# Full 128x128 weight blocks for every matmul of the routing in an mLSTM, expert and GLU kernel

## The chip, the cores and the metric

One NeuronCore of one Trainium2 chip runs the whole program. The metric is the device time in microseconds (us). Engines are named as the profile names them: PE is TensorE's matmuls, PEld its weight loads, DVE VectorE, ACT ScalarE, POOL GpSimd, SP SyncE, which issues most DMAs.

## The reference

Three steps follow one another. A gated recurrence (4 batches, 8 heads, 768 steps, head size 40) gives 3072 tokens of 320 values. Each token is then given to one of 8 experts by a greedy rule over all 3072 x 8 gate values, at most 384 tokens to an expert, and goes through that expert's two layers. A gated block follows (320 to 1536 and back).

```python
# recurrence, per head: C = f*C + i*v k^T;  n = f*n + i*k;  y = sigmoid(o) * (C q) / max(|n.q|, 1)
logits = x @ w_gate                      # 3072 x 8
for idx in np.argsort(-logits.flatten()):
    tok, e = idx // 8, idx % 8
    if assigned[tok] >= 0 or counts[e] >= 384:
        continue
    assigned[tok] = e; counts[e] += 1
for e in range(8):
    out[mask_e] = np.maximum(x[mask_e] @ w1[e], 0) @ w2[e]
return ((1 / (1 + np.exp(-(out @ w_gate2)))) * (out @ w_val)) @ w_out
```

## The kernel before, in words

The recurrence runs first, in chunks of 128 steps, in an order that a list scheduler settles. From the line `ctx.enter_context(tc.manual_schedule())` on, each engine's instructions stand in the order in which the code issues them.

**The experts** follow in the order in which they fill up (`Ffn.run(i)`, i = 0 to 7). Each works on the 384 tokens of one expert: first layer, ReLU, second layer, then twelve blocks of the gated part. Nearly all of it is fp32r matmuls with 128x128 weight blocks and 384 or 320 moving columns (lines 966 to 1084), which the rows show as f32.

**The routing** of expert i+1 (`Routing.phase`) is a generator that `drive` advances by one step at each `yield` of `Ffn.run(i)`. Its matmuls so stand between the fp32r matmuls of the expert before it. Phase 0, which has no expert to stand in, runs by itself between the recurrence and the first expert.

A phase looks for a threshold digit by digit, 6, 6, 5, 5, 5 and 5 bits (`BITS`). For each digit, DVE compares all 3072 best gate values (`v`, 128 partitions x 24) with n thresholds, n = 63 or 31 (`compare`, L547), into `cmp`, bf16. PE counts by 24 accumulating matmuls, one for each of the 24 token columns: weights `cmp[:, jj, :n]`, 128 rows and n columns, moving operand `A[:, jj, :]`, 8 columns (L602). DVE turns the counts into a 0/1 column `sat` of n rows, and one matmul with weights `ones[:n, :]` sums it for all partitions (L611). When the threshold is found, one matmul with `ones` counts (L639), five turn the tokens of the expert into a list (L669 to L674: weights `zx`, `md`, `prev` of 48 columns, then `tris` and `ones` of 128), and three gather it by a one-hot matrix `oh` of 48 rows (L694). L716 updates the counts, with `ones`.

So a phase has two blocks of 24 matmuls with 63 weight columns, four with 31, six single ones with 63 or 31 weight rows, a group of five (three in phase 7), a group of three, and L639 and L716, whose weights are 128x128.

Of the kernel before, what the change touches and what calls it, by code (L numbers as in the profile page):

```python
# [7 lines left out]
FT = mybir.dt.float32  # L8
FR = mybir.dt.float32r
BF = mybir.dt.bfloat16  # L10
F16 = mybir.dt.float16
I32 = mybir.dt.int32
# [3 lines left out]
OP = mybir.AluOpType  # L16
# [7 lines left out]
NJ = NC * B  # L24
NT = B * S
E = 8
CAP = NT // E
# [13 lines left out]
class Attention:  # L41
# [325 lines left out]
    def run(self, rt, fn):  # L367
        rt.consts()
        with self.tc.tile_pool(name="a_gate", bufs=1) as self.gp:
            self.setup()  # L370
            self.setup2()
            g1 = self.gates(1, NC)
            self.step(-1, lambda n: None)
            self.step(0, lambda n: [next(g1, 0) for _ in range(2 * n)])
            for _ in g1:
                pass
            self.step(1, lambda n: None)
            self.lambdas()
        with self.tc.tile_pool(name="a_conv", bufs=1) as cv:
            side = fn.prep_moe2(cv)  # L380
            for j in range(2, NC * NS + 1):
                self.step(j, lambda n: [next(side, 0) for _ in range(n)])
            for _ in side:
                pass
# [59 lines left out]
class Routing:  # L444
# [7 lines left out]
    def alloc(self, ctx):  # L452
        self.wk = ctx.enter_context(self.tc.tile_pool(name="r_work", bufs=1))
        self.idx = ctx.enter_context(self.tc.tile_pool(name="r_idx", bufs=2))

    def consts(self):
        nc, one = self.nc, self.one
        jp = self.g["jp"]
# [5 lines left out]
        nc.vector.memset(self.ones, 1.0)  # L464
        it = one.tile([128, 64], I32, name="it64")
        nc.gpsimd.iota(it, pattern=[[1, 64]], base=0, channel_multiplier=0)
        nb, s, self.tab = 0, 32, []
        for r, nb in enumerate(self.BITS):
            s -= nb
            n = 2 ** nb - 1  # L470
            t = one.tile([128, n], I32, name=f"tab{r}")
            nc.vector.tensor_scalar(t, it[:, 1:1 + n], s, None, op0=OP.logical_shift_left)
            self.tab.append((n, s, t))
        n, s, t = self.tab[0]
        k = one.tile([128, 2, n], I32, name="k0")
        self.sign(k[:, 0], t)
# [3 lines left out]
                       allow_small_or_imprecise_dtypes=True)  # L480
        nc.gpsimd.iota(self.we[:, 1], pattern=[[1, E]], base=0, channel_multiplier=0,
                       allow_small_or_imprecise_dtypes=True)
        self.srow = one.tile([48, CAP], F16, name="srow")
        nc.gpsimd.iota(self.srow, pattern=[[1, CAP]], base=0, channel_multiplier=0,
                       allow_small_or_imprecise_dtypes=True)
        self.scol = one.tile([128, 3], FT, name="scol")
        nc.gpsimd.iota(self.scol, pattern=[[128, 3]], base=0, channel_multiplier=1,
                       allow_small_or_imprecise_dtypes=True)
        self.GI = one.tile([48, 129], F16, name="GI")
        jc = one.tile([48, 2], FT, name="jc")  # L490
        nc.gpsimd.iota(jc[:, 0:1], pattern=[[0, 1]], base=0, channel_multiplier=1,
                       allow_small_or_imprecise_dtypes=True)
        nc.vector.tensor_scalar(jc[:, 1:2], jc[:, 0:1], float(NJ), -float(NJ), op0=OP.is_equal, op1=OP.mult)
        nc.vector.tensor_scalar(jc[:, 0:1], jc[:, 0:1], 0.0, None, op0=OP.is_gt)
        nc.vector.tensor_add(self.GI[:, 128:129], jc[:, 0:1], jc[:, 1:2])
        self.mmp = one.tile([128, 2 * NJ + 1], BF, name="mmp")
        nc.vector.memset(self.mmp[:, 0:1], 0.0)
        self.lm = one.tile([128, NJ, E], FT, name="lm")
        self.v = one.tile([128, NJ], FT, name="v")
        self.t8 = one.tile([128, NJ], FT, name="t8")  # L500
        self.A = one.tile([128, NJ, E], BF, name="A")
        self.cmp = one.tile([128, NJ, 63], BF, name="cmp")
        self.pen = one.tile([128, E], FT, name="pen")
# [40 lines left out]
    def compare(self, sl, th, n):  # L544
        v = self.v[:, sl]
        k = v.shape[1]
        self.nc.vector.tensor_tensor(self.cmp[:, sl, :n], v[:, :, None].to_broadcast([128, k, n]),  # L547
                                     th.bitcast(FT)[:, None, :].to_broadcast([128, k, n]), op=OP.is_ge)
# [8 lines left out]
    def phase(self, i, on_e, on_x):  # L557
# [13 lines left out]
        ge = wk.tile([63, E], BF, name="ge")  # L571
        sat = wk.tile([63, 1], BF, name="sat")
        tx = wk.tile([128, 1], I32, name="tx")
        h = 16
        for r, (n, s, tab) in enumerate(self.tab):
# [25 lines left out]
            for jj in range(NJ):  # L601
                nc.tensor.matmul(p[:n, :E], cmp[:, jj, :n], A[:, jj, :], start=(jj == 0), stop=(jj == NJ - 1))  # L602
            if i:
# [6 lines left out]
            p2 = self.ps(i)  # L610
            nc.tensor.matmul(p2[:, :1], self.ones[:n, :], sat[:n], start=True, stop=True)  # L611
            dig = wk.tile([128, 1], U32, name="dig", bufs=2)
# [37 lines left out]
        nc.vector.tensor_reduce(mx, es, axis=AX.X, op=OP.max)  # L650
        mm = self.mmp[:, 1:]
        zx = wk.tile([128, 2 * NJ], BF, name="zx")
        md = wk.tile([128, 2 * NJ], BF, name="md")
        nc.vector.tensor_scalar(mm[:, :NJ], self.asg, mx, None, op0=OP.is_equal)
# [13 lines left out]
        po, pk = p[:48, 128:129], p[:, 132:132 + NJ]  # L668
        nc.tensor.matmul(po, zx, self.ones[:, :1], start=True, stop=True)  # L669
        nc.tensor.matmul(p[:48, :128], md, self.tri, start=True, stop=False)  # L670
        nc.tensor.matmul(p[:48, :128], prev, self.ones, start=False, stop=True)
        if not last:
# [3 lines left out]
        gi = self.GI  # L676
        oh = wk.tile([48, CAP], F16, name="oh")
        nc.vector.tensor_copy(off, po)
        nc.vector.tensor_scalar(oh, self.srow, off, None, op0=OP.is_ge)
        nc.vector.tensor_copy(gi[:, :128], p[:48, :128])  # L680
        if not last:
# [39 lines left out]
class Ffn:  # L721
# [208 lines left out]
    def trans(self, i):  # L930
        nc, xg = self.nc, self.XG.pop(i)

        def tr(p, tb, d):
            r0, n = ROWS[d]
            nc.tensor.transpose(p[:n, tb * 128:(tb + 1) * 128], xg[:, tb, r0:r0 + n], self.g["ident"])

        if i:
            def src(d):
                p = self.mmt()[:, :CAP]
                for tb in range(3):  # L940
                    tr(p, tb, d)
                return p
        else:
            R = self.g["R"]
            ps = [self.ps.tile([128, CAP], FT, name=f"ac{d}", bufs=1) for d in range(3)]
            for tb in range(3):
                pw = self.g["rps"](1)[:, :504]
                for _ in range(WARM[tb]):
                    nc.tensor.matmul(pw, R.ones, R.cmp[:, :8, :], start=True, stop=True)
                for d in range(3):  # L950
                    tr(ps[d], tb, d)

            def src(d):
                return ps[d]
        self.XH[i] = []
        yield from self.split("x", src, self.XH[i])
        if self.padfree:
            self.widen(self.XH[i])
        else:
            self.owed = self.XH[i]  # L960
# [151 lines left out]
def tile_kernel(ctx, tc, a, out):  # L1112
    nc = tc.nc
# [3 lines left out]
    g = {}  # L1117
    g["jp"] = con.tile([128, 128], FT, name="jp")
    nc.gpsimd.iota(g["jp"], pattern=[[1, 128]], base=0, channel_multiplier=-1, allow_small_or_imprecise_dtypes=True)
    g["ident"] = con.tile([128, 128], FT, name="ident")  # L1120
    nc.vector.tensor_scalar(g["ident"], g["jp"], 0.0, None, op0=OP.is_equal)
    g["lg"] = con.tile([128, NJ, E], FT, name="lg")
# [3 lines left out]
    with ExitStack() as c2:  # L1126
        at = Attention(c2, tc, g, a, xd)
        at.run(r, fn)
    fn.alloc(ctx)
# [53 lines left out]
```

## Time and profile before

| | |
|---|---|
| median of three runs (lowest, highest) | 911.55 us (905.52, 912.48) |
| the profiled execution: time, span | 911.91 us, 910.2 us |
| granted TensorE clock, mean of the span | 0.947 of full speed |
| busy: PE, PEld, DVE, ACT, POOL | 94%, 89%, 62%, 39%, 31% |
| recurrence | 0 to 223 us of the span |
| routing phase 0, alone, clock 0.5 | 223 to 251 us |
| experts 0 to 7, clock 1.0 | 251 to 906 us |

The busy shares are means over stages of different kinds. The time itself lies about 1.7 us over the span. A clock of 1.0 is 2.4 GHz, 0.5 is 1.2 GHz.

### The profile page before, as it was taken

The numbers are of one execution on the slowest core, as the hardware profiler recorded it, in microseconds if no ns is written. First come the engines' busy times: TensorE is split into PE (matmuls) and PEld (weight loads), VectorE is DVE, ScalarE is ACT, GpSimd is POOL, SyncE is SP. The second block draws the span as 40 slices with busy tenths as digits, with TensorE's granted clock in tenths as the row PEclk, the third lists the DMA queues.
The fourth block names the chain that finished last, engine by engine and source line by source line (L and its number), as shares of the span: only waits on it lengthen the run. The fifth ranks groups of instructions, "written<-read, shape, count | busy, mean of one in ns | idle before, by whom it ended". The sixth has DMA issues, their size and how long they took to land.

```text
span 910.2 us, 16439 instructions
## 1 busy us (share of the span) xinstructions
PE 854.9 (94%) x6284; PEld 808.6 (89%) x6284; DVE 562.9 (62%) x1492; ACT 356.7 (39%) x753; POOL 281.0 (31%) x295
## 2 busy tenths in 40 slices
PE   6899798988499999999999999999999999999996
PEld 5898787988289999999999999999998999999996
DVE  7869999796765656655555565556555555542321
ACT  6498756551043251243215224422522341243321
POOL 3356676552120071044007103500720170053001
PEclk9698789797599999999999999999999999999999
DMA  6987878550130130040031005001300400060000
GB/s 123 188 191 153 194 169 178 124 142 30 38 113 1 39 111 23 1 149 23 2 112 38 23 1 150 22 2 56 94 23 1 136 30 8 1 149 23 1 1 22
DMA packets 125215, 65.64 MB, mean 72 GB/s; under 512 B 103888, under 2 KB 115344, under 8 KB 125136
## 3 DMA queue, kind: packets, MB, share of 16 engines
q1 hardware_dynamic: 122688, 56.68, 26.4%
q0 software_dynamic: 2304, 7.87, 2.7%
q8 instruction: 49, 0.80, 0.4%
q14 instruction: 30, 0.25, 0.1%
q10 hardware_dynamic: 144, 0.05, 0.0%
HBM read 56.71 MB, written 7.86 MB: 71 GB/s over the span
## 4 chain that ended last, share of the span: by engine, by line
PE 73%; DVE 6%; DMA 1%; issue 1%; POOL 1%; ACT 1%; SPq 0%; POOLq 0%; DVEq 0%; ACTq 0%
PE mm L966 8%; PE mm L968 7%; PE mm L967 7%; PE mm L988 7%; PE ac L1082 5%; PE mm L973 5%; PE mm L972 5%; PE ac L1084 5%; PE ac L1083 4%; PE rp L602 3%; PE ac L1005 3%; PE ac L1006 2%; PE ac L1007 2%; PE po L296 1%; PE ac L1011 1%
## 5 line engine op out<-in xcount | busy, mean ns | idle before, releaser
L926 POOL DMA_INDIRECT xg<-xd,ix x24 | 23.8, 993 | 399.4 <-DVE scr L697 394.6
L966 PE MATMUL mm<-yh,mh 128*128 128x384 f32 x384 | 135.1, 352 | 0.0
L967 PE MATMUL mm<-yh,ml 128*128 128x384 f32 x384 | 130.1, 339 | 0.0
L968 PE MATMUL mm<-yl,mh 128*128 128x384 f32 x384 | 130.1, 339 | 0.0
L1061 ACT ACTIVATE sg<-mm 128x384 f32<-128x384 f32 x96 | 47.1, 490 | 146.3 <-PE mm L973 146.3
L1068 DVE TENSOR_TENSOR gl<-gf,gh 128x384 fp32r<-128x384 f32 x96 | 75.5, 786 | 36.5 <-ACT gh L1074 36.0
L1074 ACT ACTIVATE gh<-gf 128x384 fp32r<-128x384 f32 x96 | 50.2, 523 | 116.2 <-DVE gf L1073 116.2
L1082 PE MATMUL ac<-oh,gh 128*128 128x320 f32 x288 | 93.2, 324 | 0.0
L1084 PE MATMUL ac<-oh,gl 128*128 128x320 f32 x288 | 89.3, 310 | 0.6 <-DVE gl L1068 0.6
L1083 PE MATMUL ac<-ol,gh 128*128 128x320 f32 x288 | 89.1, 309 | 0.0
L1073 DVE TENSOR_TENSOR gf<-sg,mm 128x384 f32<-128x384 f32 x96 | 52.7, 549 | 56.2 <-ACT sg L1061 55.4
L996 ACT ACTIVATE gh<-mm 128x384 fp32r<-128x384 f32 x64 | 31.3, 491 | 124.4 <-PE mm L973 66.7
L966 PEld LDWEIGHTS mm<-yh,mh 128*128 128x128 f32 x384 | 72.3, 188 | 0.8
L967 PEld LDWEIGHTS mm<-yh,ml 128*128 128x128 f32 x384 | 72.3, 188 | 0.0
L968 PEld LDWEIGHTS mm<-yl,mh 128*128 128x128 f32 x384 | 72.2, 188 | 0.0
L972 PE MATMUL mm<-y,m 128*128 128x384 f32 x192 | 65.1, 339 | 0.0
L973 PE MATMUL mm<-pad,mr 128*128 128x384 f32 x192 | 65.0, 338 | 0.0
L249 PE MATMUL s<-qT,kb 120*128 120x128 f32 x384 | 60.0, 307 | 3.4 <-DVE ee L250 3.2
L238 ACT ACTIVATE ee<-pg,GT 128x128 f32<-128x128 f32 x192 | 54.3, 404 | 14.4 <-PE po L296 9.9
L249 PEld LDWEIGHTS s<-qT,kb 120*128 120x128 f32 x384 | 53.8, 216 | 5.3 <-DVE ee L250 4.5
L296 PE MATMUL po<-vn,ee 128*128 128x41 f32 x384 | 56.6, 310 | 0.0
L296 PEld LDWEIGHTS po<-vn,ee 128*128 128x128 f32 x384 | 55.8, 227 | 0.2 <-DVE t L306 0.2
(278 smaller groups left out, 2056.7 us busy)
## 6 DMA issues: line engine op xcount, KB each, us to landing
ws<-in_moe_w_dram SPq DMA_DIRECT2D x15, 480.0 KB, 6.8
ws<-in_moe_w_dram SPq DMA_DIRECT2D x14, 512.0 KB, 4.2
ws<-in_moe_w_dram SPq DMA_DIRECT2D x18, 256.0 KB, 5.6
on<-in_o_gate_dram SPq DMA_DIRECT2D x24, 160.0 KB, 3.9
xd<-x SPq DMA_DIRECT2D x24, 160.0 KB, 2.9
st<-in_moe_w_out_dram SPq DMA_DIRECT2D x12, 320.0 KB, 3.0
st<-in_moe_w_gate_dram SPq DMA_DIRECT2D x8, 384.0 KB, 4.7
st<-in_moe_w_val_dram SPq DMA_DIRECT2D x8, 384.0 KB, 3.4
```

What stands on the lines that cost most here:

```text
L249: nc.tensor.matmul(s[:, h, :], self.KB[:, a, r, :], self.QT[j][:, a, :], start=True, stop=True)
L296: nc.tensor.matmul(self.PO[j][:, 4 * k + h, :], w[:, h, :], self.VN[s][:, 4 * k + h, :], start=True, stop=True)
L966: mm(p, wh[:, d, cs], h[:, d], start=(d == 0), stop=False)
L967: mm(p, wl[:, d, cs], h[:, d], start=False, stop=False)
L968: mm(p, wh[:, d, cs], l[:, d], start=False, stop=False)
L972: mm(p, w2[:, cs], x[2], start=False, stop=False)
L973: mm(p, wr[:, c2], self.pad[z], start=False, stop=True)
L988: mm(p, (self.al if t == 1 else self.ah)[:, d, cs], x[t // 2][:, d], start=(d == 0 and t == 0), stop=False)
L1068: nc.vector.tensor_tensor(gl, hs[f - 1][0], hs[f - 1][1].bitcast(FT), op=OP.subtract)
L1082: mm(o, gh[:, ts], self.oh[:, k], start=(k == 0), stop=False)
L1083: mm(o, gh[:, ts], self.ol[:, k], start=False, stop=False)
L1084: mm(o, gl[:, ts], self.oh[:, k], start=False, stop=(k == 11))
```

## The change

Every matmul of the routing gets weights of 128 rows and 128 columns.

- `cmp` becomes a flat tile of 23 x 63 + 128 columns. `compare` packs the n results of each token column without a gap, and the weights of matmul jj are the 128 columns from jj x n on: its own n, then those of the next token columns, at the end zeros or what an earlier digit left there. The rows of the result from n on are not read.
- `sat` becomes a kept tile of 128 rows for each n, zero from n on, and its matmul takes the whole of `ones`.
- `zx`, `md`, `mmp`, `GI` and `oh` become kept tiles with 128 columns or rows, zero where the routing writes nothing.
- Some constants move to another pool (`jp`, `it`, `k`), which makes room in the memory.

Four memsets join DVE's start (`GI`, a wider `mmp`, two `sat`; one narrow one goes), one POOL's start (`cmp`), and three POOL's work at the end of the recurrence (`zx`, `md`, `oh`).

```diff
@@ -452,8 +452,13 @@
     def alloc(self, ctx):
         self.wk = ctx.enter_context(self.tc.tile_pool(name="r_work", bufs=1))
         self.idx = ctx.enter_context(self.tc.tile_pool(name="r_idx", bufs=2))
-
-    def consts(self):
+        self.oh = self.wk.tile([128, CAP], F16, name="oh")
+        self.zx = self.wk.tile([128, 128], BF, name="zx")
+        self.md = self.wk.tile([128, 128], BF, name="md")
+        for t in (self.zx, self.md, self.oh):
+            self.nc.gpsimd.memset(t, 0.0)
+
+    def consts(self, tmp):
         nc, one = self.nc, self.one
         jp = self.g["jp"]
         self.tri = one.tile([128, 128], BF, name="tri")
@@ -486,20 +491,25 @@
         self.scol = one.tile([128, 3], FT, name="scol")
         nc.gpsimd.iota(self.scol, pattern=[[128, 3]], base=0, channel_multiplier=1,
                        allow_small_or_imprecise_dtypes=True)
-        self.GI = one.tile([48, 129], F16, name="GI")
+        self.GI = one.tile([128, 129], F16, name="GI")
+        nc.vector.memset(self.GI, 0.0)
         jc = one.tile([48, 2], FT, name="jc")
         nc.gpsimd.iota(jc[:, 0:1], pattern=[[0, 1]], base=0, channel_multiplier=1,
                        allow_small_or_imprecise_dtypes=True)
         nc.vector.tensor_scalar(jc[:, 1:2], jc[:, 0:1], float(NJ), -float(NJ), op0=OP.is_equal, op1=OP.mult)
         nc.vector.tensor_scalar(jc[:, 0:1], jc[:, 0:1], 0.0, None, op0=OP.is_gt)
-        nc.vector.tensor_add(self.GI[:, 128:129], jc[:, 0:1], jc[:, 1:2])
-        self.mmp = one.tile([128, 2 * NJ + 1], BF, name="mmp")
-        nc.vector.memset(self.mmp[:, 0:1], 0.0)
+        nc.vector.tensor_add(self.GI[:48, 128:129], jc[:, 0:1], jc[:, 1:2])
+        self.mmp = one.tile([128, 128], BF, name="mmp")
+        nc.vector.memset(self.mmp, 0.0)
         self.lm = one.tile([128, NJ, E], FT, name="lm")
         self.v = one.tile([128, NJ], FT, name="v")
         self.t8 = one.tile([128, NJ], FT, name="t8")
         self.A = one.tile([128, NJ, E], BF, name="A")
-        self.cmp = one.tile([128, NJ, 63], BF, name="cmp")
+        self.cmp = one.tile([128, (NJ - 1) * 63 + 128], BF, name="cmp")
+        nc.gpsimd.memset(self.cmp[:, NJ * 63:], 0.0)
+        self.sat = {n: one.tile([128, 1], BF, name=f"sat{n}") for n in (63, 31)}
+        for t in self.sat.values():
+            nc.vector.memset(t, 0.0)
         self.pen = one.tile([128, E], FT, name="pen")
         nc.vector.memset(self.pen, 0.0)
         self.act = one.tile([128, NJ], FT, name="act")
@@ -544,7 +554,8 @@
     def compare(self, sl, th, n):
         v = self.v[:, sl]
         k = v.shape[1]
-        self.nc.vector.tensor_tensor(self.cmp[:, sl, :n], v[:, :, None].to_broadcast([128, k, n]),
+        cmp = self.cmp[:, :NJ * n].rearrange("p (j n) -> p j n", n=n)
+        self.nc.vector.tensor_tensor(cmp[:, sl], v[:, :, None].to_broadcast([128, k, n]),
                                      th.bitcast(FT)[:, None, :].to_broadcast([128, k, n]), op=OP.is_ge)
 
     def start(self, c):
@@ -569,7 +580,6 @@
         T = wk.tile([128, 63], I32, name="T")
         Q = wk.tile([128, 63], I32, name="Q")
         ge = wk.tile([63, E], BF, name="ge")
-        sat = wk.tile([63, 1], BF, name="sat")
         tx = wk.tile([128, 1], I32, name="tx")
         h = 16
         for r, (n, s, tab) in enumerate(self.tab):
@@ -599,7 +609,8 @@
                 yield
             p = self.ps(i)
             for jj in range(NJ):
-                nc.tensor.matmul(p[:n, :E], cmp[:, jj, :n], A[:, jj, :], start=(jj == 0), stop=(jj == NJ - 1))
+                nc.tensor.matmul(p[:, :E], cmp[:, jj * n:jj * n + 128], A[:, jj, :], start=(jj == 0), stop=(jj == NJ - 1))
+            sat = self.sat[n]
             if i:
                 nc.vector.tensor_tensor(ge[:n], p[:n, :E], self.rem[:n], op=OP.is_ge)
                 nc.vector.tensor_reduce(sat[:n], ge[:n], axis=AX.X, op=OP.max)
@@ -608,7 +619,7 @@
                                         accum_out=sat[:n])
             yield
             p2 = self.ps(i)
-            nc.tensor.matmul(p2[:, :1], self.ones[:n, :], sat[:n], start=True, stop=True)
+            nc.tensor.matmul(p2[:, :1], self.ones, sat, start=True, stop=True)
             dig = wk.tile([128, 1], U32, name="dig", bufs=2)
             dg = dig.bitcast(I32)
             nc.vector.tensor_scalar(dig, p2[:, :1], float(2 ** s), None, op0=OP.mult)
@@ -648,9 +659,8 @@
         nc.vector.tensor_tensor(es, p[:, 0:E], self.rem, op=OP.is_ge)
         nc.vector.tensor_tensor(es, es, self.we[:, 0], op=OP.mult)
         nc.vector.tensor_reduce(mx, es, axis=AX.X, op=OP.max)
-        mm = self.mmp[:, 1:]
-        zx = wk.tile([128, 2 * NJ], BF, name="zx")
-        md = wk.tile([128, 2 * NJ], BF, name="md")
+        mm = self.mmp[:, 1:2 * NJ + 1]
+        zx, md = self.zx[:, :2 * NJ], self.md[:, :2 * NJ]
         nc.vector.tensor_scalar(mm[:, :NJ], self.asg, mx, None, op0=OP.is_equal)
         nc.vector.scalar_tensor_tensor(mm[:, NJ:], t8, mx, td, op0=OP.is_equal, op1=OP.mult)
         prev = self.mmp[:, :2 * NJ]
@@ -666,18 +676,18 @@
         yield
         p = self.ps(i)
         po, pk = p[:48, 128:129], p[:, 132:132 + NJ]
-        nc.tensor.matmul(po, zx, self.ones[:, :1], start=True, stop=True)
-        nc.tensor.matmul(p[:48, :128], md, self.tri, start=True, stop=False)
-        nc.tensor.matmul(p[:48, :128], prev, self.ones, start=False, stop=True)
+        nc.tensor.matmul(p[:, 128:129], self.zx, self.ones[:, :1], start=True, stop=True)
+        nc.tensor.matmul(p[:, :128], self.md, self.tri, start=True, stop=False)
+        nc.tensor.matmul(p[:, :128], self.mmp, self.ones, start=False, stop=True)
         if not last:
             nc.tensor.matmul(pk, self.tris, mm[:, NJ:], start=True, stop=False)
             nc.tensor.matmul(pk, self.ones, zx[:, NJ:], start=False, stop=True)
         off = wk.tile([48, 1], FT, name="off")
         gi = self.GI
-        oh = wk.tile([48, CAP], F16, name="oh")
+        oh = self.oh
         nc.vector.tensor_copy(off, po)
-        nc.vector.tensor_scalar(oh, self.srow, off, None, op0=OP.is_ge)
-        nc.vector.tensor_copy(gi[:, :128], p[:48, :128])
+        nc.vector.tensor_scalar(oh[:48], self.srow, off, None, op0=OP.is_ge)
+        nc.vector.tensor_copy(gi[:48, :128], p[:48, :128])
         if not last:
             eq = wk.tile([128, NJ], FT, name="eq")
             nc.vector.scalar_tensor_tensor(eq, pk, float(CAP), mm[:, NJ:], op0=OP.is_lt, op1=OP.mult)
@@ -946,7 +956,7 @@
             for tb in range(3):
                 pw = self.g["rps"](1)[:, :504]
                 for _ in range(WARM[tb]):
-                    nc.tensor.matmul(pw, R.ones, R.cmp[:, :8, :], start=True, stop=True)
+                    nc.tensor.matmul(pw, R.ones, R.cmp[:, :504], start=True, stop=True)
                 for d in range(3):
                     tr(ps[d], tb, d)
 
@@ -1115,16 +1125,16 @@
     dr = ctx.enter_context(tc.tile_pool(name="dr", bufs=1, space=bass.MemoryType.DRAM))
     xd = dr.tile([NT, HD], FT, name="xd")
     g = {}
-    g["jp"] = con.tile([128, 128], FT, name="jp")
-    nc.gpsimd.iota(g["jp"], pattern=[[1, 128]], base=0, channel_multiplier=-1, allow_small_or_imprecise_dtypes=True)
     g["ident"] = con.tile([128, 128], FT, name="ident")
-    nc.vector.tensor_scalar(g["ident"], g["jp"], 0.0, None, op0=OP.is_equal)
     g["lg"] = con.tile([128, NJ, E], FT, name="lg")
     fn = Ffn(tc, g, a, xd, out, con)
     fn.alloc_moe2()
     r = g["R"] = Routing(tc, g, con)
     with ExitStack() as c2:
         at = Attention(c2, tc, g, a, xd)
+        g["jp"] = at.one.tile([128, 128], FT, name="jp")
+        nc.gpsimd.iota(g["jp"], pattern=[[1, 128]], base=0, channel_multiplier=-1, allow_small_or_imprecise_dtypes=True)
+        nc.vector.tensor_scalar(g["ident"], g["jp"], 0.0, None, op0=OP.is_equal)
         at.run(r, fn)
     fn.alloc(ctx)
     r.alloc(ctx)
```

Every matmul and load stands where it stood on PE. At one digit with n = 31, PE's rows before are these; `yl`, `mh` and their like belong to the gated part of the expert:

```order
L968 MATMUL mm<-yl,mh_66 128x384
L602 LDWEIGHTS cmp
L602 MATMUL rp<-A,cmp 31x8
...
L966 MATMUL mm<-yh,mh_67 128x384
L967 MATMUL mm<-yh,ml_69 128x384
...
L973 MATMUL mm<-pad_2711,mr 128x384
L611 LDWEIGHTS ones
L611 MATMUL rp<-sat,ones 128x1
L1082 MATMUL ac_3295<-oh,gh 128x320
```

And now:

```order
L978 MATMUL mm<-yl,mh_63 128x384
L612 LDWEIGHTS cmp
L612 MATMUL rp<-A,cmp 128x8
...
L976 MATMUL mm<-yh,mh_64 128x384
L977 MATMUL mm<-yh,ml_66 128x384
...
L983 MATMUL mm<-pad_2717,mr 128x384
L622 LDWEIGHTS ones
L622 MATMUL rp<-sat_131,ones 128x1
L1092 MATMUL ac_3302<-oh,gh 128x320
```

Nothing moved; the result of the counting matmuls has 128 rows in place of 31 or 63. Line numbers from 611 on are some 10 higher in the changed file.

On DVE the start of the program changes. Before:

```order
L464 MEMSET ones 128x128
L497 MEMSET mmp 128x1
L504 MEMSET pen 128x8
L506 MEMSET act 128x24
L508 MEMSET rem 128x8
L510 MEMSET asg 128x24
L1121 TENSOR_SCALAR ident<-jp 128x128
```

And now:

```order
L469 MEMSET ones 128x128
L495 MEMSET GI 128x129
L503 MEMSET mmp 128x64
L512 MEMSET sat_130 128x1
L512 MEMSET sat_131 128x1
L514 MEMSET pen 128x8
L1137 TENSOR_SCALAR ident<-jp 128x128
```

The memsets of `act`, `rem` and `asg` have moved behind the constants that follow, still ahead of the gates of the recurrence.

## Rows read from the trace of the kernel before

**Rows 1.** Engines' busy time in one stretch; columns: stretch, its length, busy, clock, DMA, GB/s.

```profile
350.00:425.00 75.00, 75.00 (x543) 70.89 (x542) 44.56 (x125) 25.84 (x48) 20.93 (x19) 1.00 0.17 53
```

**Rows 2.** Waits of PE, 262 to 905 us; columns: total, times, longest.

```profile
PE mm L935 <- DMA xg<-xd,ix: 0.8, 1, 0.8
PE ac L1084 <- DVE gl L1068: 0.6, 1, 0.6
```

**Rows 3.** Timeline of PE around one L639, weights 128x128; columns: start, length, instructions.

```profile
547.86 0.34 PE L973 MATMUL mm<-pad,mr 128*128 128x384 f32 x1
548.04 0.18 PE L639 MATMUL rp<-sm,ones 128*128 128x8 bf16 x1
...
548.46 0.31 PE L1084 MATMUL ac<-oh,gl 128*128 128x320 f32 x1
```

**Rows 4.** Timeline of PE around one L611, weights 31 rows by 128.

```profile
304.33 0.34 PE L973 MATMUL mm<-pad,mr 128*128 128x384 f32 x1
304.61 0.17 PE L611 MATMUL rp<-sat,ones 31*128 31x1 bf16 x1
...
305.11 0.31 PE L1084 MATMUL ac<-oh,gl 128*128 128x320 f32 x1
```

**Rows 5.** Timeline of PE around one block of 31 columns.

```profile
301.15 0.34 PE L968 MATMUL mm<-yl,mh 128*128 128x384 f32 x1
...
301.68 0.34 PE L968 MATMUL mm<-yl,mh 128*128 128x384 f32 x1
301.95 0.76 PE L602 MATMUL rp<-A,cmp 128*31 128x8 bf16 x24
...
303.10 0.34 PE L968 MATMUL mm<-yl,mh 128*128 128x384 f32 x1
```

**Rows 6.** Timeline of PE around one block of 63 columns.

```profile
278.48 0.34 PE L968 MATMUL mm<-yl,mh 128*128 128x384 f32 x1
278.74 0.93 PE L602 MATMUL rp<-A,cmp 128*63 128x8 bf16 x24
...
280.07 0.34 PE L968 MATMUL mm<-yl,mh 128*128 128x384 f32 x1
```

**Rows 7.** Timeline of PE around one group L669 to L674.

```profile
315.45 0.31 PE L1083 MATMUL ac<-ol,gh 128*128 128x320 f32 x1
315.59 0.30 PE L1084 MATMUL ac<-oh,gl 128*128 128x320 f32 x1
...
315.93 0.22 PE L671 MATMUL rp<-ones,mmp 128*48 128x128 bf16 x1
316.08 0.19 PE L673 MATMUL rp<-mmp,tris 128*128 128x24 bf16 x1
316.12 0.17 PE L674 MATMUL rp<-zx,ones 128*128 128x24 bf16 x1
...
316.58 0.34 PE L968 MATMUL mm<-yl,mh 128*128 128x384 f32 x1
```

**Rows 8.** Timeline of PE at an fp32r matmul with 64 weight columns.

```profile
351.46 0.34 PE L1010 MATMUL ac<-gl,bh 128*64 128x384 f32 x1
351.63 0.34 PE L1011 MATMUL ac<-gh,bh 128*128 128x384 f32 x1
```

**Rows 9.** Weight loads by shape, 262 to 905 us; columns: busy us, mean ns, idle before.

```profile
L602 PEld LDWEIGHTS <-cmp 128*31 128x31 bf16 x672 | 18.6, 94 | 7.0 <-DVE gf L1073 3.8 <-issue 3.2
L602 PEld LDWEIGHTS <-cmp 128*63 128x63 bf16 x336 | 11.8, 113 | 3.5 <-issue 2.0 <-DVE gl L997 1.5
...
L639 PEld LDWEIGHTS <-ones 128*128 128x128 bf16 x7 | 0.7, 97 | 1.1 <-issue 1.1
```

**Rows 10.** Timeline of phase 0, the second digit, clock 0.5.

```profile
228.10 1.80 DVE L547 TENSOR_TENSOR cmp<-v,T 128x1008 bf16<-128x1008 f32 x2
...
229.36 1.44 PE L602 MATMUL mm<-A,cmp 128*63 128x8 bf16 x24 [2.22 <-DVE cmp L547]
```

**Rows 11.** Timeline of DVE at the program's start.

```profile
0.93 0.17 DVE L464 MEMSET ones<- 128x128 bf16 x1 [0.93 <-PEq L1170]
```

More of the change, by code (lines that the diff above doesn't have):

```diff
@@ L367, in run @@
     def run(self, rt, fn):
-        rt.consts()
+        rt.consts(self.one)
         with self.tc.tile_pool(name="a_gate", bufs=1) as self.gp:
@@ L464, in consts @@
         nc.vector.memset(self.ones, 1.0)
-        it = one.tile([128, 64], I32, name="it64")
+        it = tmp.tile([128, 64], I32, name="it64")
         nc.gpsimd.iota(it, pattern=[[1, 64]], base=0, channel_multiplier=0)
@@ L474, in consts @@
         n, s, t = self.tab[0]
-        k = one.tile([128, 2, n], I32, name="k0")
+        k = tmp.tile([128, 2, n], I32, name="k0")
         self.sign(k[:, 0], t)
```

## The prediction

> **What bounds the kernel now.** I read the busy time by stage first, then PE's waits, then PE's timeline around single routing matmuls, and the weight loads by shape. From the first expert on PE is the bound: in 75 us between 350 and 425 it is busy for 75.00 at clock 1.0, DVE for 44.56 [rows 1]. Between 262 and 905 us PE has three waits of over 0.1 us, the two longest 0.8 and 0.6 us [rows 2]. So in this stage a nanosecond taken from PE's stream comes off the end, as long as nothing new makes PE wait. The routing's matmuls lie in that stream in small insertions, and what one costs is read from the fp32r matmuls on both sides: the time from the last one before it to the third one behind it, less what these steps take without it. A step with 384 moving columns takes 0.177 us (301.15 to 301.68 is three of them [rows 5]), one with 320 takes 0.145 (315.45 to 315.59 [rows 7]). I go to the third because the first one behind starts early on the record and waits for its weights.
>
> **A full block against a small one.** Two single matmuls stand between the same neighbours, L973 ahead and L1082, L1083, L1084 behind. With L639, whose weights are already 128x128, L973 to L1084 takes 0.60 us [rows 3]; with L611, whose weights have 31 rows, 0.78 [rows 4]. The steps alone make 0.177 + 2 x 0.145 = 0.467. So the full one costs 0.13 and the small one 0.31, though both move 8 columns or fewer. The 0.18 between them lies on both sides: L611 starts 0.28 after its neighbour where L639 starts 0.18 after it, and the rest is lost behind. PE does not fetch the weights of a small block beneath the matmul ahead, nor the next large weights beneath the small matmul.
>
> A block of 24 fits the same picture. With 31 columns, 301.68 to 303.10 less 0.53 is 0.89 us; its 24 matmuls run 0.76, less the 0.17 of the last one, over 23 gaps: 0.026 a step [rows 4, 5]. 0.31 + 23 x 0.026 is 0.91. With 63 columns the cost is 1.59 - 0.53 = 1.06 and the step (0.93 - 0.17) / 23 = 0.033 [rows 6]. The stall is a price for each insertion, the step one for each load.
>
> **What the change takes away, part by part.** Seven phases lie in the stream; phase 0 comes below.
>
> L611, 42 of them: 0.31 becomes 0.13, as L639 has it: 42 x 0.18 = 7.6 us.
>
> The blocks of 24: the stall falls to 0.13, and the step becomes that of 128-column bf16 loads. That step is the one unknown that matters. The nearest rows are L673 and L674, two such loads in a row: their starts lie 0.04 apart, and their ends 0.02 (316.08 + 0.19 and 316.12 + 0.17) [rows 7]. The first waits for its own load within its length, so the ends tell the step better. The load itself lasts 97 ns at 128 columns, 94 at 31 and 113 at 63 [rows 9]: a full load is like the 31-column one. I take 0.026, and keep 0.020 to 0.040 as ends. A block then costs 0.13 + 23 x 0.026 = 0.73 us. That is 0.33 less for 63 columns and 0.16 less for 31: 14 x 0.33 + 28 x 0.16 = 4.6 + 4.5 = 9.1 us. With 0.020 it would be 15; with 0.040 a loss of 4, since a block would cost 1.05.
>
> The groups L669 to L674, six of them: the way in loses its share of the stall, about 0.09, and so does the change from 48 to 128 columns inside, where L671 to L673 takes 0.15 [rows 7] for 128 moving columns that need about 0.06: 6 x 0.18 = 1.1, and 0.2 for the short group of phase 7. The seven groups L694 have small weights on the way in and out, like L611: 7 x 0.18 = 1.3.
>
> Phase 0 runs alone at clock 0.5, as a chain from DVE to PE and back, so only what lies on the chain counts. Its second digit shows it: the block of 63 runs 1.44 us, (1.44 - 0.17) / 23 = 0.055 a step, and starts at 229.36, while the second half of the comparison lands at 228.10 + 1.80 = 229.90 [rows 10]. With steps of 0.026 to 0.03, PE would wait for that half and then do its last 8 loads, ending near 230.3 in place of 230.80: 0.45 saved, and about as much at the first digit. The four 31-column digits keep their step. I count 0.9 (0 to 1.5). The transfers of the first expert's weights are issued after phase 0, so they move with it.
>
> **What it adds.** DVE's start takes three memsets more and one wider. The largest comparable memset takes 0.17 us [rows 11]; four would be 0.7 at most, but they overlap, and the first of them runs while POOL still makes `jp`. I take 0.2 on the path, 0 to 0.7. POOL's memset of 65 columns stands ahead of constants that the recurrence needs later; I count nothing, and under 0.1 us if that is wrong. POOL's three at the end of the recurrence write before phase 0 needs these tiles: nothing, at worst a few tenths. Packing `cmp` leaves DVE's element count as it is. The two halves of a comparison and the matmuls that read past their own columns keep their order, and no step is moved on any queue.
>
> Does PE gain a wait? The time between the counting block and L611, and from L611 to the next block, shrinks by 0.18 us each; PE shows no wait for a comparison or for `sat` in this stage now, and DVE has 40% of it free [rows 1, 2]. I count nothing.
>
> **The sum.** 7.6 + 9.1 + 1.3 + 1.3 + 0.9 - 0.2 = 20.0 us. Against the profiled execution's 911.9 that gives 891.9; the median of the runs is 0.4 lower, so 891.5.
>
> **Two rules weighed.** An fp32r matmul with 64 weight columns, L1010, is followed by one with 128 after 0.17 us, and shows no stall [rows 8]. The Trainium skill, "TensorEngine Tiling (Array Packing)", section Key Properties, says that changing the tiling mode drains TensorE. L611 agrees, L1010 does not. By the rule every small block here owes its stall to its size, and the whole 0.18 goes each time; since L1010 escapes it, some other property may be at work, and the third rival below keeps its chance.
>
> A full bf16 load lasts 97 ns beside 94 for 31 columns [rows 9]. The Trainium skill, "TensorE: Matmul & The Clock Gate", section LDWEIGHTS, gives columns / 1.2 ns for a load, that is 107 ns at 128 columns beside 26 at 31, which speaks against widening. Its section on the weight-path modes excepts full loads of 128 columns that are not FP32, and the row agrees with the exception. Without the exception, and with 0.107 us a step, a block would cost 0.13 + 23 x 0.107 = 2.6 us, an estimate from that page, and the kernel would be some 58 us slower than before.
>
> **The rivals.**
>
> *The wide loads step slower than the narrow ones,* at 0.033 to 0.040 us. For it: the starts of L673 and L674 lie 0.04 apart, and the weights of the new blocks begin at odd columns of a 2-byte tile, which no full load of the rows shows. Against: their ends. At 0.033 the blocks gain 2.4 us in place of 9.1, and the time is 898; at 0.040 they lose 4.3, and it is 905.
>
> *The load's price goes by columns, and the kernel gets slower.* From 31 to 63 columns a load grows by 19 ns [rows 9], 0.6 ns a column; 65 columns more than 63 make 0.033 + 0.039 = 0.072 a step. A block would cost 1.79, the 42 of them 75.0 in place of 14 x 1.06 + 28 x 0.89 = 39.8: 35.2 lost, 10.9 won elsewhere, 936 us. The place is the same 42 blocks; it decides from 0.047 us a step, where (39.8 + 10.9) / 42 = 1.21 = 0.13 + 23 x 0.047. The 97 ns of L639 speak against it.
>
> *Short weight rows are not what stalls L611.* Its load is 128 columns wide already. If its stall and L694's come from something else that L639 lacks, 7.6 + 1.3 us stay: 900. Against: the two stand between the same neighbours, and rows are the difference left.
>
> *The won time turns into waits* of PE for DVE or ACT, whose work between two insertions does not shrink. If half is lost: 901. Against: PE waits for neither now [rows 2].
>
> **How the numbers follow.** Forecast 0.75; slower steps 0.12; price by columns 0.03; rows not the cause 0.05; waits 0.05. The three runs before lie 7 us apart, so some 3.5 us either way belong to any median; with the 0.020 end the forecast reaches down to 885. Upward the range takes in 898, 900 and 901, to 903. A measurement here can tell about 1%, 9 us, from no change. Faster by over 1%, under 902.4, are the forecast, most of the slower steps and nearly all of the next two: 0.92. Within 1%: 0.05. Slower: 0.03.
>
> **What would show it.** L973 to L1084 around the single matmul on `sat` takes 0.60; blocks of 24 run about 0.76 from first start to last end for either n, and start 0.18 after their neighbour; an expert takes some 2.7 us less than before; PE still shows no wait on a comparison. A step above 0.035 in the blocks, or a start still 0.27 after the neighbour, makes the prediction wrong.

## The result, and the profile after

The change makes the kernel faster. The median after is 889.92 us (888.73 to 891.06, 6 runs), before 912.37 (905.52 to 919.14, 6 runs). The ratio is that of the means of the fast runs, which leaves out the 919.14: 0.9764, with a 95% interval of 0.9728 to 0.98. The forecast was 891.5 in a range of 885 to 903. The profiled execution of after took 888.73 us with a span of 887.0, against 911.9 and 910.2 before. Line numbers of after are some 10 higher: L602 is L612, L611 is L622, L639 is L650, L669 to L674 are L679 to L684, L694 is L704, L966 to L968 are L976 to L978, L972 and L973 are L982 and L983, L1082 to L1084 are L1092 to L1094.

First PE's timeline of after, around a block of 24 for 63 thresholds, one for 31, a single matmul on `sat` and a group. The columns are start, length, instructions.

```profile
279.96 0.34 PE L978 MATMUL mm<-yl,mh 128*128 128x384 f32 x1
280.14 0.76 PE L612 MATMUL rp<-A,cmp 128*128 128x8 bf16 x24
...
281.18 0.34 PE L978 MATMUL mm<-yl,mh 128*128 128x384 f32 x1
...
301.18 0.34 PE L978 MATMUL mm<-yl,mh 128*128 128x384 f32 x1
301.36 0.76 PE L612 MATMUL rp<-A,cmp 128*128 128x8 bf16 x24
...
302.41 0.34 PE L978 MATMUL mm<-yl,mh 128*128 128x384 f32 x1
...
303.62 0.34 PE L983 MATMUL mm<-pad,mr 128*128 128x384 f32 x1
303.80 0.18 PE L622 MATMUL rp<-sat,ones 128*128 128x1 bf16 x1
303.84 0.39 PE L1092 MATMUL ac<-oh,gh 128*128 128x320 f32 x1
304.07 0.31 PE L1093 MATMUL ac<-ol,gh 128*128 128x320 f32 x1
304.22 0.31 PE L1094 MATMUL ac<-oh,gl 128*128 128x320 f32 x1
...
384.04 0.34 PE L983 MATMUL mm<-pad,mr 128*128 128x384 f32 x1
384.22 0.18 PE L679 MATMUL rp<-ones,zx 128*128 128x1 bf16 x1
...
384.39 0.17 PE L684 MATMUL rp<-zx,ones 128*128 128x24 bf16 x1
...
384.79 0.30 PE L1094 MATMUL ac<-oh,gl 128*128 128x320 f32 x1
```

Both kinds of block now look alike: they start 0.18 after their neighbour, and run 0.76 from first start to last end. From L978 ahead to the third matmul behind is 1.22 and 1.23 us, where it was 1.59 and 1.42 [rows 5, 6]. The single matmul takes 0.60 from L983 to L1094, as the one with full weights did before, and not 0.78 [rows 3, 4]. The group of five takes 0.75 between such neighbours, 0.28 beyond the steps; at the place shown before it took 0.99 less 0.145 + 2 x 0.177, so 0.49 [rows 7].

The waits of PE between 255 and 885 us, and its load groups and busy time, in that order, each of after. In the loads the columns are busy us, mean ns, idle before.

```profile
PE mm L726 <- DVE sm L638: 1.7, 1, 1.7
PE ac L1094 <- DVE gl L1078: 0.7, 1, 0.7
PE mm L945 <- DMA xg<-xd,ix: 0.4, 1, 0.4
PE mm L998 <- ACT xh L916: 0.3, 1, 0.3
```

```profile
L612 PEld LDWEIGHTS <-cmp 128*128 128x128 bf16 x1008 | 28.1, 96 | 6.5 <-issue 4.4 <-DVE gf L1083 1.1 <-DVE gl L1007 1.0
L622 PEld LDWEIGHTS <-ones 128*128 128x128 bf16 x42 | 4.0, 96 | 6.6 <-issue 5.7 <-DVE gf L1083 0.9
```

```profile
350.00:425.00 75.00, 75.00 (x580) 72.04 (x579) 44.15 (x125) 26.02 (x49) 20.93 (x19) 1.00 0.17 53
```

No matmul in the stream waits for a comparison or for `sat`. A full load of 128 columns lasts 96 ns, against 113 with 63 columns and 94 with 31 [rows 9]. PE is as busy as before in the same 75 us, and does 580 matmuls in them where it did 543 [rows 1]. Most of that is one counting block more; of the large fp32r ones, 384 or 320 columns wide, 410 start there in place of 397. The first wait in the list is new, and lies ahead of the first block of the stream; it comes up again below.

The rest of the difference is best read by stages. This table is worked out from the timelines of the traces, in us. It has the start of the first counting block, and then times that each run on from the one before: to L704 (L694 before), to the first expert's first matmul (L998), to L726, to the first block in the stream, to the last matmul of the last block in it, and to the last matmul of all.

| kernel | first block at | to L704 | to L998 | to L726 | to the stream | stream | tail |
|---|---|---|---|---|---|---|---|
| before | 224.16 | 21.82 | 8.33 | 13.37 | 11.08 | 508.22 | 114.73 |
| after | 223.66 | 21.06 | 9.88 | 14.60 | 10.91 | 485.71 | 112.68 |
| e1, small weights | 221.10 | 21.90 | 8.30 | 14.03 | 10.99 | 505.00 | 113.24 |
| e2, small `sat` | 225.66 | 21.02 | 9.78 | 14.68 | 10.91 | 492.41 | 113.83 |
| e4, 127 columns | 226.04 | 31.81 | 9.81 | 13.52 | 10.90 | 517.32 | 112.73 |
| e5, 96 rows | 225.88 | 21.05 | 9.66 | 14.72 | 10.95 | 485.41 | 112.67 |
| e8, `jp` moved | 224.03 | 21.82 | 9.43 | 14.30 | 11.01 | 508.88 | 114.10 |
| after again | 226.06 | 21.08 | 9.36 | 13.49 | 10.90 | 486.53 | 112.69 |
| e15, more fillers | 225.94 | 21.05 | 8.28 | 14.61 | 10.91 | 485.71 | 112.69 |

The stream and the tail give 22.5 and 2.05 us, phase 0 gives 0.76, and between L704 and L726 2.8 are lost. The first column scatters by 5 us among kernels whose work up to there hardly differs, so it says nothing on the change.

### The profile page after: what moved, and what is told of

It reads as the page before. It is cut to its first block, busy times and chain, and to the rows that moved or that the text cites. A ratio compares the mean times of both kernels' runs of the same rounds, so it can differ in the third digit from the quotient of the medians.

```text
span 887.0 us, 16455 instructions
## 1 busy us (share of the span) xinstructions
PE 829.3 (93%) x6284; PEld 794.4 (90%) x6284; DVE 565.3 (64%) x1495; ACT 356.3 (40%) x753; POOL 281.4 (32%) x299
## 4 chain that ended last, share of the span: by engine, by line
PE 77%; DVE 14%; issue 3%; ACT 3%; DMA 1%; POOL 1%; POOLq 0%; DVEq 0%; SPq 0%; ACTq 0%
PE mm L976 8%; PE mm L977 7%; PE mm L978 7%; PE mm L998 7%; PE ac L1092 5%; PE mm L983 5%; PE mm L982 5%; PE ac L1094 5%; PE ac L1093 5%; PE rp L612 3%; PE ac L1015 3%; PE ac L1017 2%; PE ac L1016 2%; PE po L296 2%; DVE t L752 2%
## 5 line engine op out<-in xcount | busy, mean ns | idle before, releaser
L976 PE MATMUL mm<-yh,mh 128*128 128x384 f32 x384 | 134.1, 349 | 0.0
L978 PE MATMUL mm<-yl,mh 128*128 128x384 f32 x384 | 129.1, 336 | 0.0
L1078 DVE TENSOR_TENSOR gl<-gf,gh 128x384 fp32r<-128x384 f32 x96 | 77.4, 807 | 37.1 <-ACT gh L1084 36.9
L1084 ACT ACTIVATE gh<-gf 128x384 fp32r<-128x384 f32 x96 | 50.2, 523 | 114.5 <-DVE gf L1083 114.5
L1092 PE MATMUL ac<-oh,gh 128*128 128x320 f32 x288 | 92.6, 321 | 0.0
L1094 PE MATMUL ac<-oh,gl 128*128 128x320 f32 x288 | 89.1, 310 | 0.7 <-DVE gl L1078 0.7
L976 PEld LDWEIGHTS mm<-yh,mh 128*128 128x128 f32 x384 | 72.4, 189 | 0.2 <-DVE xl L917 0.2
L978 PEld LDWEIGHTS mm<-yl,mh 128*128 128x128 f32 x384 | 72.2, 188 | 0.0
L983 PE MATMUL mm<-pad,mr 128*128 128x384 f32 x192 | 64.8, 337 | 0.0
L982 PE MATMUL mm<-y,m 128*128 128x384 f32 x192 | 64.5, 336 | 0.0
L1094 PEld LDWEIGHTS ac<-oh,gl 128*128 128x128 f32 x288 | 54.1, 188 | 0.9 <-DVE gl L1078 0.9
L1106 POOL DMA_INDIRECT out_dram<-xg,ix x24 | 24.9, 1039 | 94.4 <-ACT xg L1104 90.8
```

What stands on the lines that cost most here:

```text
L976: mm(p, wh[:, d, cs], h[:, d], start=(d == 0), stop=False)
L978: mm(p, wh[:, d, cs], l[:, d], start=False, stop=False)
L982: mm(p, w2[:, cs], x[2], start=False, stop=False)
L983: mm(p, wr[:, c2], self.pad[z], start=False, stop=True)
L1078: nc.vector.tensor_tensor(gl, hs[f - 1][0], hs[f - 1][1].bitcast(FT), op=OP.subtract)
L1092: mm(o, gh[:, ts], self.oh[:, k], start=(k == 0), stop=False)
```

## The experiments

**Only the weights undone (e1).** Everything of the change stays, memory, memsets and packed columns, but every matmul takes its small weights again.

```diff
-nc.tensor.matmul(p[:, :E], cmp[:, jj * n:jj * n + 128], ...)
+nc.tensor.matmul(p[:n, :E], cmp[:, jj * n:jj * n + n], ...)
-nc.tensor.matmul(p2[:, :1], self.ones, sat, ...)
+nc.tensor.matmul(p2[:, :1], self.ones[:n, :], sat[:n], ...)
 (L679 to L681: po, zx; p[:48], md; p[:48], prev)
 (L704: oh[:48, ...], gi[:48])
```

> The changed kernel with its memory, its memsets and its packed comparison, but every routing matmul with the small weights of the kernel before (31 or 63 columns, 31 or 63 rows, 48 columns, 48 rows). If the size of the weights is what saves, the insertions cost 60 to 61 us again, as before, in place of some 40, and the time is 909 to 911. If the new places of the tiles in memory make fp32r steps of the gated part 0.174 us in place of 0.177 (seen in the changed kernel's trace), that stays here and the time is 906 to 908. Rival, that memory and packing do all of it: 890.

Measured: 906.4 us (903.31 to 912.32, 4 runs), a ratio of 0.9952, 0.9903 to 1.0. The insertions cost what they did before. Summed over all of them after 262 us (time to the third fp32r matmul behind, less the steps) they are 60.8 us before, 60.7 in e1, 40.1 after: the 20.6 us belong to the full weights. But the stream and the tail of e1 are 4.7 us shorter than before's with the same insertions, and that the weights can't explain. PE's timeline of e1 at one `sat` matmul, stalled as in [rows 4]:

```profile
305.24 0.34 PE L978 MATMUL mm<-yl,mh 128*128 128x384 f32 x1
305.51 0.17 PE L622 MATMUL rp<-sat,ones 31*128 31x1 bf16 x1
...
306.07 0.34 PE L978 MATMUL mm<-yl,mh 128*128 128x384 f32 x1
```

**Only the single matmul small (e2), and with 96 rows (e5).** Both change one line of after, and tell whether rows cause its stall.

```diff
-nc.tensor.matmul(p2[:, :1], self.ones, sat, start=True, stop=True)
+nc.tensor.matmul(p2[:, :1], self.ones[:n, :], sat[:n], ...)     # e2
+nc.tensor.matmul(p2[:, :1], self.ones[:96, :], sat[:96], ...)   # e5
```

> The changed kernel, but the single matmul on sat takes only the 31 or 63 rows that it needs, by 128 columns. If few rows stall as few columns do, each of the 42 costs 0.30 us in place of 0.13 and starts 0.27 after its neighbour in place of 0.18: 897. Rival, that only columns matter: 890.

> The changed kernel, but the single matmul on sat takes 96 rows (sat is zero from row 31 or 63 on). If the stall comes from the array being divided, into 32 or 64 rows, 96 rows have no such division and cost 0.13 as 128 do: 890. Rival, that any missing row stalls: 897.

Measured: e2 897.8 us (893.73 to 898.51; ratio 0.984, 0.9803 to 0.9878), e5 889.23 (886.59 to 891.18; ratio 0.9754, 0.9716 to 0.9791). PE's timeline of e2, then of e5:

```profile
301.12 0.34 PE L983 MATMUL mm<-pad,mr 128*128 128x384 f32 x1
301.39 0.17 PE L622 MATMUL rp<-sat,ones 31*128 31x1 bf16 x1
...
301.89 0.31 PE L1094 MATMUL ac<-oh,gl 128*128 128x320 f32 x1
```

```profile
300.81 0.34 PE L983 MATMUL mm<-pad,mr 128*128 128x384 f32 x1
300.99 0.18 PE L622 MATMUL rp<-sat,ones 96*128 96x1 bf16 x1
...
301.41 0.31 PE L1094 MATMUL ac<-oh,gl 128*128 128x320 f32 x1
```

With 31 rows L622 starts 0.27 after its neighbour and the passage takes 0.77; with 96 rows it starts after 0.18 and takes 0.60, as with 128. Over all 42 the cost beyond the steps is 0.30 each in e2 and 0.128 in e5 and after, so these insertions are 7.2 of the 7.9 us by which e2's stream and tail are longer than after's. The rows are the cause, and the weights need not have 128 of them.

**127 columns in the blocks (e4).** One column less than a full load; nothing else in the block differs.

```diff
-nc.tensor.matmul(p[:, :E], cmp[:, jj * n:jj * n + 128], ...)
+nc.tensor.matmul(p[:127, :E], cmp[:, jj * n:jj * n + 127], ...)
```

> The changed kernel, but the counting blocks load 127 columns in place of 128; the counts that are read are the same. It parts the stall from the load. If a full tile removes the stall and exactly 128 columns make the load quick, a block still starts 0.18 after its neighbour, but its step grows from 0.026 to about 0.06 (0.033 at 63 columns and 64 columns more at one for each cycle of 2.4 GHz): a block 1.5 us in place of 0.70, and the time 923. Rival, that a load of 127 columns is as quick as one of 128: 890.

Measured: 931.33 us (925.38 to 932.36), a ratio of 1.0204, 1.016 to 1.0248: slower than before. PE's timeline and its load group in e4:

```profile
299.07 0.34 PE L978 MATMUL mm<-yl,mh 128*128 128x384 f32 x1
299.25 1.52 PE L612 MATMUL rp<-A,cmp 128*127 128x8 bf16 x24
...
301.06 0.34 PE L978 MATMUL mm<-yl,mh 128*128 128x384 f32 x1
```

```profile
L612 PEld LDWEIGHTS <-cmp 128*127 128x127 bf16 x1008 | 65.6, 139 | 1.6
```

The block still starts 0.18 after its neighbour, so it has no stall; but it runs 1.52, a step of (1.52 - 0.17) / 23 = 0.059 where 128 columns take 0.026, and its loads last 139 ns where they last 96. The mean block costs 1.455 where after's costs 0.70: 42 x 0.755 = 31.7, and the stream is 31.6 longer. In phase 0, at clock 0.5, the six blocks together cost another 10.75, which the 923 expected left out. So stall and step have separate causes: a nearly full block is enough against the stall, and not against the slow step.

**Even starts (e6).** One idle column for each token column, so that every load begins at an even column. `cmp` grows with it and is cleared as a whole, and what lies behind it moves by 32 bytes.

```diff
-cmp[:, jj * n:jj * n + 128]
+cmp[:, jj * (n + 1):jj * (n + 1) + 128]
```

> The changed kernel with an idle column behind each token column of the comparison, so that every 128-column load begins at an even column, on 4 bytes. If a load from an odd column costs nothing, the step of a block stays 0.0257 us and the time 889 to 892; if odd starts are slower, the step falls below 0.0257 on average, by up to 0.001 us for each nanosecond that they cost, halved.

Measured: 889.83 us in one run; a block costs 0.70. PE's timeline of e6:

```profile
279.85 0.76 PE L612 MATMUL rp<-A,cmp 128*128 128x8 bf16 x24
```

It is the same 0.76 as after, so the odd start of a 2-byte column costs nothing, and the prediction's ground for slower wide loads falls.

**Where the rest of the stream's gain comes from (e8, e9, e13, e11).** The fp32r matmuls themselves step closer after the change. PE's timeline of before, and of after, between two fp32r matmuls ten steps apart:

```profile
381.81 0.34 PE L967 MATMUL mm<-yh,ml 128*128 128x384 f32 x1
...
383.58 0.34 PE L968 MATMUL mm<-yl,mh 128*128 128x384 f32 x1
```

```profile
381.61 0.34 PE L977 MATMUL mm<-yh,ml 128*128 128x384 f32 x1
...
383.34 0.34 PE L978 MATMUL mm<-yl,mh 128*128 128x384 f32 x1
```

1.77 against 1.73: from L967 to L968 the mean step is 176.8 ns before and 173.6 after, and e1 has 173.6 with its small weights. That leaves memory, since the change takes `jp` and two scratch tiles out of the permanent pool and puts others in, so that what is allocated behind them moves. e8 is before with `jp` alone moved to the pool of the attention; e9 is after with 512 idle bytes where `jp` was; e13 and e11 move only the work tiles of after, from which the fp32r matmuls take their moving operands, by 64 and 32 bytes.

```diff
-    g["jp"] = con.tile([128, 128], FT, name="jp")            # e8, from before
+        g["jp"] = at.one.tile([128, 128], FT, name="jp")
+    g["hole"] = con.tile([128, 128], FT, name="hole")        # e9, with a memset
-        self.spacer = wp.tile([1, 1], FT, name="spacer")
+        self.spacer = wp.tile([1, 17], FT, name="spacer")[:, :1]   # e13; e11: 9
```

> The kernel before, with jp alone moved to the recurrence's pool as the changed kernel has it, and nothing else. The gated part's weights lie where the changed kernel has them, its moving operands stay 96 past a multiple of 128 bytes. If the weights' place set the step of L967 to L968, it is 0.174; if the moving operands' place does, it stays near 0.177, and all insertions cost 60 to 61 us.

> The changed kernel with 512 idle bytes ahead of all kept tiles, where jp lay before: the gated part's weights lie where they lay in the kernel before, while its moving operands keep their place within 128 bytes (32 past a multiple; in the kernel before 96 past). If the place of the weights makes the fp32r step of L967 to L968 0.177 us before and 0.174 after the change, it is 0.177 again; if the place of the moving operands within 128 bytes does it, it stays 0.174.

> The changed kernel with 64 idle bytes behind the expert's weights: only the work tiles move, among them the moving operands of all fp32r matmuls, to 96 past a multiple of 128 bytes, as in the kernel before; the weights stay. If the moving operands' place within 128 bytes sets the step, L967 to L968 is 0.177; if not, 0.174.

> The changed kernel with 32 idle bytes in the same place: the moving operands begin at a multiple of 64 bytes. If their place sets the step, it becomes at most 0.174, and perhaps shorter than in either kernel: 886 to 890. If the place is of no account: 889 to 890, with a step of 0.174.

Measured: e8 913.79 us, e9 894.04 and e13 886.6, one run each; e11 891.34 (889.45 to 892.64; ratio 0.9799, 0.9752 to 0.9847). What tells here is the mean step, not the total, since the recurrence ahead scatters by more. It is 176.8 in e8, 173.6 in e9, 174.6 in e13 and 175.2 in e11. PE's timeline of e8 over ten such steps shows 1.77 again:

```profile
384.30 0.34 PE L967 MATMUL mm<-yh,ml 128*128 128x384 f32 x1
...
386.07 0.34 PE L968 MATMUL mm<-yl,mh 128*128 128x384 f32 x1
```

Moving `jp` changes nothing, and putting the gated part's weights back where they lay changes nothing: it isn't their place. Moving the work tiles alone does change the step, by 1 to 2 ns, so their place is at least one cause. The moving operands of L966 to L968 begin at byte 96 of 128 before and in e8, at 32 after and in e9, and those steps go together; but e13, at 96 again, comes back only a third of the way. Counted within 256 bytes the kernels do sort: before and e8 begin at 224, after and e9 at 32, e13 at 96, e11 at 64, and e6, which also begins at 64, has 175.2 as e11 has. So all seven would fit a price by the place within 256 bytes. That isn't shown: no run moves after's tiles to 224, and why one place costs more than another is left open. Its price is 4.7 us between before and e1 by one profile of each; between before and after 3.9 us are left for it beside the insertions.

**More fillers before the first expert (e10, e15), and after itself again (e14).** After loses 1.55 us between L704 and the first expert. The clock is granted in full later there. PE's timeline and windows (columns as in rows 1) of before, then the same of after; L945 (L935 before) transposes the first expert's tokens:

```profile
246.38 3.54 PE L949 MATMUL rp<-cmp,ones 128*128 128x504 bf16 x8
251.74 0.52 PE L935 MATMUL ac<-ident,xg 128*128 128x128 f32 x3 [1.82 <-issue]
```

```profile
247.00:250.00 3.00, 2.92 (x7) 0.76 (x5) 1.38 (x10) 0.89 (x2) 2.11 (x2) 0.50 0.76 243
250.00:253.00 3.00, 1.26 (x8) 0.85 (x9) 1.07 (x2) 0.81 (x2) 1.23 (x1) 0.92 0.68 185
```

```profile
245.03 3.57 PE L959 MATMUL rp<-cmp,ones 128*128 128x504 bf16 x8
251.06 0.87 PE L945 MATMUL ac<-ident,xg 128*128 128x128 f32 x3 [2.47 <-issue]
```

```profile
250.00:253.00 3.00, 1.94 (x8) 1.37 (x9) 0.69 (x1) 0.65 (x2) 0.85 (x2) 0.50 0.32 86
253.00:256.00 3.00, 2.67 (x14) 2.14 (x13) 1.36 (x3) 1.86 (x5) 0.68 (x2) 0.83 0.34 85
```

Before, the eight idle matmuls of `WARM` end at 249.9, and a mean of 0.92 over 250 to 253 puts the rise from 1.2 to 2.4 GHz at 250.5. After, they end at 248.6, PE is idle until 251.06, the stretch up to 253 stays at 0.50, and 0.83 in the next puts the rise at 254.0. The longer pause alone doesn't explain that, as e8 shows:

```profile
246.25 3.54 PE L949 MATMUL rp<-cmp,ones 128*128 128x504 bf16 x8
251.71 0.87 PE L935 MATMUL ac<-ident,xg 128*128 128x128 f32 x3 [1.91 <-issue]
```

```profile
253.00:256.00 3.00, 2.65 (x12) 1.91 (x12) 0.75 (x2) 1.24 (x4) 1.18 (x3) 0.73 0.19 49
```

Its eight begin and end within 0.13 us of those of before, its pause is 0.1 longer, and its clock rises at 254.6. More idle matmuls would still bridge the pause:

```diff
-WARM = (8, 2, 1)
+WARM = (12, 2, 1)
```

> The changed kernel with 12 idle matmuls ahead of the first expert's transposes in place of 8, which do not change the result. In the changed kernel's trace the clock rises to 1.0 only at 254 us, 9 us after the first of the 8, in the kernel before 4 us after it. If the shorter phase 0 lost its gain because the 8 now end before the clock rises, 12 bring the rise to about 250 us, the first expert's matmuls start 8.3 us after L694's counterpart in place of 9.9, and the time is 887 to 888. Rival, that the weights' transfers set the start: 890.

> The changed kernel once more, beside the next one on the same chip, as the measure for it: 889 to 892.

> The changed kernel with 12 idle matmuls in place of 8 once more. Its profile had 2.3 us less from the first counting block to the end, 661.0 in place of 663.3, but a longer recurrence. If that is a gain, the median is 2 us under the changed kernel's on this chip; if other runs lose it again, the two agree within 1 us.

The windows of e10:

```profile
250.00:253.00 3.00, 2.40 (x9) 0.94 (x8) 1.40 (x2) 1.26 (x2) 1.54 (x2) 0.71 0.82 225
253.00:256.00 3.00, 2.64 (x18) 1.99 (x16) 1.10 (x3) 2.25 (x5) 1.54 (x3) 1.00 0.06 22
```

The clock is back at 251.7, 4.9 us after L704 and no longer 9.3 (5.9 in e15), and the first expert starts 8.09 and 8.28 us after L704 in e10 and e15, as before the change. The total doesn't show it: e10 891.79 us (888.52 to 896.65; ratio 0.9817, 0.9762 to 0.9872), e15 889.0 (885.22 to 891.29; 0.9748, 0.971 to 0.9786), after again 889.95 (886.5 to 891.18; 0.9754, 0.9717 to 0.9791). Two runs of one kernel lie 2.8 us apart, after lies between them, and a gain of 1.5 can't be told. The late rise isn't the full blocks' doing: e8, whose weights are those of before, has it too and starts its first expert after 9.43 us; e1, with the same small weights, starts it after 8.30. And the bridge doesn't help L726, which still comes 14.07 and 14.61 us later.

## Why the prediction was right

**The single matmuls and the groups.** 42 x 0.18 = 7.6 was forecast, 0.30 less 0.128 gives 7.2. The groups gave 1.45 where 1.3 was forecast, those of L694 1.6 where it was 1.3. The reading by two single matmuls between the same neighbours held to a few hundredths, and e2 priced it alone.

**The blocks.** 9.1 was forecast; they cost 39.7 before and 29.4 after, 10.3 less. The unknown step came out at (0.76 - 0.17) / 23 = 0.0257, and a block costs 0.70 where 0.73 was forecast. Going by the ends of L673 and L674, 0.02 apart, and not by their starts, 0.04 apart, was right. All insertions together are 20.7 less, 19.3 was the sum of these terms.

**The rivals.** Slower wide loads: false, by 0.0257 and by e6. A price by columns: false at 128 columns, but true one column below, where e4 has a step of 0.059 and a total of 931, on the far side of the point of 0.047 that the prediction gave. Rows not the cause: false, by e2 and e5. Won time turned into waits: false in the stream, where PE waits for no comparison.

**The two rules weighed.** The stall comes with 31 or 63 rows (0.30) and is gone with 96 or 128 (0.13). The Trainium skill, "TensorEngine Tiling (Array Packing)", section Key Properties, has the change of tiling mode drain TensorE, and its section Available Configurations lists 32, 64 and 128 rows. The runs agree with that, 96 rows behaving like 128. L1010, with 64 weight columns in fp32r and no stall [rows 8], still doesn't fit, and no run here tells why. The load of 127 columns costs 0.033 us a step more than that of 128. That agrees with the exception for 128 columns that are not FP32 in the Trainium skill, "TensorE: Matmul & The Clock Gate", section on the weight-path modes.

**What the steps missed.** Two things, of opposite sign. The steps of the fp32r matmuls were taken as unchanged, and with them the place of the tiles in memory as of no account; they gave about 3.9 us: the stream and the tail gained 24.6, the insertions 20.7. And phase 0's gain was counted through to the end. Its own size was near, 0.76 for 0.9: at the second digit the block runs 1.02 us at clock 0.5, where it ran 1.44 [rows 10]. This is PE's timeline of after there, and at L726:

```profile
228.43 1.02 PE L612 MATMUL mm<-A,cmp 128*128 128x8 bf16 x24 [2.22 <-DVE cmp L558]
...
269.23 0.17 PE L726 MATMUL mm<-sm,ones 128*128 128x8 bf16 x1 [1.71 <-DVE sm L638]
```

But behind phase 0 the first expert came 1.55 us later, and L726 another 1.2, with a wait of 1.7 on DVE. Around it the chain of weights is late: SP's queue waits 2.2 us on DVE for a buffer (1.0 before), and the next conversion on ACT waits 3.3 us for that transfer. The prediction said that the first expert's transfers move with phase 0; it did not ask what the fillers and the clock do when the stage ahead ends earlier. But e8, with the weights of before, runs just as late: 2.2 and 3.6 us at those two places, and 1.5 at L716, which is L726's counterpart. Runs of one kernel differ here too (after again loses 0.1 where after loses 1.2). So no run ties this loss to the change, and what part of it belongs there stays open. That the two misses have opposite signs is luck; together they are why the profiled execution, 23.2 us shorter, comes near the sum of 20.0: 24.6 and 0.8 gained, 2.8 lost on the way to L726, and 0.7 in the recurrence's scatter and the stretch behind L726. The 0.2 for DVE's start can't be read from the time, since the recurrence scatters by more; in the trace DVE's first work on `jp`, `ident`, starts at 1.25 us in place of 1.21.

## What to carry to other kernels

A small bf16 or fp16 matmul between large ones (here fp32r, at full clock) should be given weights of 128 columns and 96 or more rows, filled up with zeros, or with columns whose results nobody reads: the stall of some 0.17 us on each insertion goes, and 128 columns load as fast as 31; 127 are the worst size tried. To price such an insertion, measure from the matmul ahead to the third behind, and look in the trace for one of the wanted shape between the same neighbours. After a change of memory, compare the step of untouched matmuls as well, or its effect is put down to the edit.

## What the runs showed of the hardware

- One column decides: bf16 loads of 128 x 128 follow each other every 0.026 us and last 96 ns, those of 128 x 127 every 0.059 and 139 ns, at full clock.
- A load may begin at an odd 2-byte column at no cost, 0.76 us a block in either case.
- The step of an fp32r matmul with 384 moving columns lies between 173.6 and 176.8 ns, by where tiles lie in memory. Over the stream and the tail that made 4.7 us (before against e1).
- Eight idle matmuls don't bring the clock back at a fixed time: begun at 246.38 the rise came at 250.5, begun at 246.25 (e8) at 254.6, begun at 245.03 at 254.0. With twelve it came 4.7 and 5.7 us after the first (e10, e15).
